# Attention and channel mix on one core: long-row tiles loaded by one transfer in place of two, with a new order of tasks

## Chip, core and metric

The kernel runs on one core of a Trainium2 chip. The metric is the device time of one execution in microseconds. A core has TensorE (PE, with its weight loads listed apart as PEld), VectorE (DVE), ScalarE (ACT), GpSimd (POOL) and the queue of SyncE (SP), which issues the DMAs of this kernel, and 16 DMA engines.

## The reference

Attention over blocks of 64 rows, then an RWKV channel mix, for 8 batches, 8 heads, 576 rows and heads of 64, so that a row of all heads has 512 columns:

```python
def _attn_ref(q, k, v):                      # each (8, 8, 576, 64)
    scores = scale * np.matmul(q, k.transpose(0, 1, 3, 2))
    scores = np.where(block_i >= block_j, scores, -1e9)
    attn = np.exp(scores - max) / (sum + 1e-09)
    return np.matmul(attn, v)
# heads side by side give x (8, 576, 512)
def _moe_ref(x, mu_k, mu_r, w_k, w_v, w_r):
    x_prev = x moved down by one row, a zero row first
    xk = mu_k * x + (1 - mu_k) * x_prev
    xr = mu_r * x + (1 - mu_r) * x_prev
    k = np.maximum(xk @ w_k, 0)              # 512 -> 1024
    v = k * k @ w_v                          # 1024 -> 512
    r = 1 / (1 + np.exp(-(xr @ w_r)))
    return r * v
```

## The kernel before

**Tiling.** Attention goes batch by batch (b = 0 to 7), the channel mix over nine chunks c of 512 rows of all batches together, so that chunk 0 needs batch 0 alone and chunk 1 batches 0 and 1.

**Long rows.** Scores need q and k turned, with the 64 columns of a head on partitions. For batches 0 to 3 (`LONGS = 4`) q and k come in as *long rows*: a partition takes nine successive rows of one head, 9 x 64 floats or 2304 bytes that lie together in DRAM, so 64 partitions hold a head. A tile `t_ld` of 128 partitions holds two heads (y = 0 on partitions 0 to 63, y = 1 on 64 to 127). `add_long` loads it, a cast to bf16 puts it into `t_nl` (two loads, x = 0 and 1, side by side), and `add_long_qkt` turns it on TensorE (line 389, task `qt`) and copies it from PSUM into `t_qkt` (task `ev`). Batches 4 to 7 load q and k in runs of 256 bytes and turn them by DMA (`turn`, line 311).

**Which heads share a tile.** In batch 0 a tile's heads are neighbours in DRAM (4g + 2x and the next), so its 128 rows of 2304 bytes are one run and it is loaded by one transfer. In batches 1 to 3 they are heads 2g + x and 4 + 2g + x, four heads apart (`heads(b)`), since their scores and values are arranged in another way; each tile is loaded by two transfers to 64 partitions each. A long-row task `longld b g n x` (n = 0 for q, 1 for k) is one tile: 8 a batch, 32 in all.

**Order.** Nothing is ordered by the compiler. The program adds 1212 tasks, each with the engines that could do it; the string `ORDER` lists them by number in the order in which they are issued, and `PLACE` gives the engine of each that has a choice (D, A, P for DVE, ACT, POOL). Both came from a planner outside the kernel, which had a cost for each task. Each engine does its tasks in that order and waits in place where data or a buffer is missing. `+n` behind a number puts n matmuls ahead of the task that nobody reads (`unread`, line 260), to fill a wait of TensorE.

**Buffers and queues.** All loads and stores are issued by SP (line 232 for loads, 899 for stores), in the order of `ORDER`. `t_ld` has 8 buffers, which long rows, weights and the q and k of later batches share; `t_nl` and `t_vl` (values) have 4 each. A buffer comes free when its cast is done. The DMAs' completions go round over eight semaphores, so that an issue waits until the one eight before it has landed.

**In order of time.** SP issues batch 0's long rows and values, then batch 1's long rows mixed with the 20 weight loads (`wld`) and batch 1's values, then batch 2's and batch 3's long rows with values, the first stores and the first loads of batch 4. On TensorE the turn of a batch (`qt`) is followed by its scores (`sc`, line 524), which alternate with the channel mix of the chunk before (`pk` line 814, `pr` 853, `pv` 880), and by its products with the values (`av`, line 616).

Of the kernel before, what the change touches and what calls it, by code (L numbers as in the profile page):

```python
# [14 lines left out]
LONGS = 4  # L15

ORDER = """
# [67 lines left out]
"""  # L85

PLACE = (
    "DAPADDPDDPDDPPADDADDAPPPPAADDAAAADAADDADDDPDDPDPPPPPPDPPDDADDPAAAPAPPP"
    "PPDAAAAAADAAPDPAPPPAAPAPPPDAAAADAADPADPPPPPPAPDAPAPAAADDAAAPAADAAAPPAA"
    "DADAPDAAAPADDPDPPAAPDDADDPPAADDPPPDADPADPAAAAPAADPAADPPPPAPDPPAAPDPAPA"  # L90
    "AAPDADDDPDAAPDADADPAPDDDPDAAAAADPAPDADPDPAADPDDDAAADPDAAAAADPAAADADDPD"
    "AADAADAAADPADDPDAAPAADPDAAAAPAADDAPDDDPAPAADDADADADADADADADADAPADAPAPA"
    "PAPADAD"
)


# [36 lines left out]
def kernel(  # L133
# [13 lines left out]
    B, H, S, D = q.shape  # L147
# [89 lines left out]
    def flex(key, alts, fn, deps, takes=(), uses=()):  # L237
        return add(key, {e: None for e in alts}, fn, deps, takes, uses)
# [91 lines left out]
    JT = S // D  # L330
# [11 lines left out]
    def add_long(b, g):  # L342
        for n, src in enumerate((q, k)):
            nb = plan.buf("nl")
            tiles["nbbuf", b, g, n] = nb
            cast["qk", b, g, n] = []
            for x in range(2):
                ld = plan.buf("ld")
                key = ("ld", b, g, n, x)
                t = load(f"longld {b} {g} {n} {x}", key,  # L350
                         lambda: new("ld", [P, S], FP),
                         lambda d, src=src, x=x: [
                             (d[y * D:y * D + D], src[b, 4 * y + 2 * g + x]
                              .rearrange("(p j) d -> p (j d)", j=JT))
                             for y in range(2)] if b else [
                             (d, src[b, 4 * g + 2 * x:4 * g + 2 * x + 2]
                              .rearrange("y (p j) d -> (y p) (j d)", j=JT))],
                         takes=[ld])

                def fn(eng, me, n=n, key=key, x=x):  # L360
                    if x == 0:
                        tiles["nb", b, g, n] = new("nl", [P, JT, P], BF)
                    convert(eng, tiles["nb", b, g, n][:, :, x * D:x * D + D],
                            tiles[key][:, :].rearrange("p (j d) -> p j d", d=D))
                cast["qk", b, g, n].append(flex(
                    f"long {b} {g} {n} {x}", ANY, fn,
                    [t] + cast["qk", b, g, n], takes=[] if x else [nb],
                    uses=[ld] + ([nb] if x else [])))
# [624 lines left out]
```

## Time and profile before

| | us |
|---|---|
| median of 3 runs | 279.02 |
| range of 3 runs | 277.21 to 281.06 |
| the profiled execution | 280.93 |
| its span, first to last instruction | 278.8 |
| PE busy | 258.6 (93%) |
| DVE busy | 205.3 (74%) |
| ACT busy | 198.9 (71%) |
| POOL busy | 79.8 (29%) |
| DMA packets, share of 16 engines' span | 76.2% |

All durations come from the profiled execution. The slices of the page are 1/40 of the span each, and their digits tenths of busy time; PEclk is the granted clock of TensorE in tenths, with a mean of 0.976. A busy engine is not always one at its best, since matmuls are pipelined and their ends modelled. The chain of waits goes back from the last instruction to what released it; "SPq" in it is SP's queue issuing.

### The profile page before, as it was taken

The numbers are of one execution on the slowest core, as the hardware profiler recorded it, in microseconds if no ns is written. First come the engines' busy times: TensorE is split into PE (matmuls) and PEld (weight loads), VectorE is DVE, ScalarE is ACT, GpSimd is POOL, SyncE is SP. The second block draws the span as 40 slices with busy tenths as digits, with TensorE's granted clock in tenths as the row PEclk, the third lists the DMA queues.
The fourth block names the chain that finished last, engine by engine and source line by source line (L and its number), as shares of the span: only waits on it lengthen the run. The fifth ranks groups of instructions, "written<-read, shape, count | busy, mean of one in ns | idle before, by whom it ended". The sixth has DMA issues, their size and how long they took to land.

```text
span 278.8 us, 9043 instructions
## 1 busy us (share of the span) xinstructions
PE 258.6 (93%) x3787; PEld 134.3 (48%) x3787; DVE 205.3 (74%) x396; ACT 198.9 (71%) x292; POOL 79.8 (29%) x112
## 2 busy tenths in 40 slices
PE   8998689987998889989997998999999999999995
PEld 8765565533434443444353444544544355444443
DVE  2467796875775848987978899789799869972232
ACT  2698859958895679959995798668969965560530
POOL 4133104833355211430152214122732021100520
PEclk9999959997999979999999999999999999999999
DMA  7958999977799896999899988999987201203003
GB/s 227 245 122 243 225 248 235 261 208 227 229 255 213 175 205 145 245 156 199 213 206 164 227 228 183 189 225 205 226 161 176 78 2 40 114 0 115 38 30 121
DMA packets 110633, 48.82 MB, mean 175 GB/s; under 512 B 99201, under 2 KB 99457, under 8 KB 110593
## 3 DMA queue, kind: packets, MB, share of 16 engines
q1 hardware_dynamic: 110592, 48.26, 76.2%
q8 instruction: 29, 0.48, 0.7%
q14 instruction: 12, 0.09, 0.1%
HBM read 33.56 MB, written 9.44 MB: 154 GB/s over the span
## 4 chain that ended last, share of the span: by engine, by line
PE 70%; DMA 9%; SPq 5%; DVE 5%; ACT 4%; issue 3%; POOL 2%; POOLq 0%; ACTq 0%; DVEq 0%
PE t_mm L814 19%; PE t_mm L880 17%; PE t_mm L853 9%; PE t_s L616 9%; PE t_s L524 6%; DMA t_ld<-in_q_dram 6%; SPq L232 5%; PE t_mm L260 4%; PE t_s L389 2%; PE t_s L260 2%; ACT t_e L555 2%; DMA t_tl<-in_k_dram 2%; POOL t_k L838 1%; DMA t_vl<-in_v_dram 1%; ACT t_qkt L243 1%
## 5 line engine op out<-in xcount | busy, mean ns | idle before, releaser
L555 ACT ACTIVATE t_e<-t_s 128x1024 f16<-128x1024 f32 (+1 forms) x96 | 89.1, 980 | 11.1 <-PE t_s L524 8.5
L880 PE MATMUL t_mm<-WV,t_k 128*128 128x512 f16 (+1 forms) x296 | 70.2, 386 | 0.1
L814 PE MATMUL t_mm<-t_xk,WK 128*128 128x512 f16 x288 | 68.5, 379 | 0.6 <-DVE t_o L891 0.3
L838 POOL TENSOR_TENSOR t_k<-t_kr 128x512 f16<-128x512 f32 x26 | 28.3, 1099 | 66.5 <-ACT t_kr L826 35.8
L880 PEld LDWEIGHTS <-t_k 128*128 128x128 f16 x296 | 28.0, 100 | 36.3 <-issue 8.6
L861 ACT ACTIVATE t_t<-t_mm 128x512 f32<-128x512 f32 x36 | 21.4, 594 | 30.7 <-PE t_mm L853 29.4
L814 PEld LDWEIGHTS <-WK 128*128 128x128 f16 x288 | 26.4, 97 | 34.6 <-issue 5.6
L891 DVE SCALAR_TENSOR_TENSOR t_o<-t_t,t_mm 128x512 f32<-128x512 f32 (+1 forms) x37 | 24.7, 667 | 17.6 <-PE t_mm L880 14.5
L853 PE MATMUL t_mm<-WR,t_xr 128*128 128x512 f16 x144 | 36.2, 380 | 0.0
L826 ACT ACTIVATE t_kr<-t_mm 128x512 f32<-128x512 f32 x40 | 23.9, 597 | 13.1 <-PE t_mm L814 12.9
L828 DVE TENSOR_SCALAR t_kr<-t_mm 128x512 f32<-128x512 f32 x32 | 21.7, 685 | 8.0 <-PE t_mm L814 7.5
L616 PE MATMUL t_s<-t_e,VO 64*32 64x64 f16 (+7 forms) x1120 | 21.9, 284 | 4.9 <-issue 3.7
L524 PE MATMUL t_s<-t_qkt 64*64 64x512 bf16 (+7 forms) x560 | 25.8, 293 | 0.6 <-ACT t_e L555 0.6
L786 DVE SCALAR_TENSOR_TENSOR t_xr<-t_d,MUR,XT 128x384 f16<-128x384 f32 (+7 forms) x42 | 24.1, 584 | 0.2
L260 PEld LDWEIGHTS <-identb 128*128 128x128 bf16 x267 | 19.2, 113 | 7.5 <-issue 5.6
L838 DVE TENSOR_TENSOR t_k<-t_kr 128x512 f16<-128x512 f32 x21 | 16.2, 781 | 8.0 <-ACT t_kr L826 7.7
L616 PEld LDWEIGHTS <-VO 64*32 64x32 f16 x1120 | 16.0, 92 | 11.9 <-issue 7.5
L786 DVE SCALAR_TENSOR_TENSOR t_xk<-t_d,MUK,XT 128x192 f16<-128x192 f32 (+7 forms) x42 | 21.2, 523 | 0.0
L731 DVE TENSOR_TENSOR XT<-t_s,t_rt 128x512 f32<-128x512 f32 x28 | 18.5, 681 | 3.1 <-PE t_s L616 3.0
L853 PEld LDWEIGHTS <-t_xr 128*128 128x128 f16 x144 | 13.0, 98 | 15.7 <-issue 1.7
L754 POOL TENSOR_TENSOR t_d<-XT 128x576 f32<-128x576 f32 x10 | 11.9, 1191 | 30.3 <-DVE XT L731 11.9
L524 PEld LDWEIGHTS <-t_qkt 64*64 64x64 bf16 x560 | 11.1, 106 | 17.3 <-issue 15.2
(67 smaller groups left out, 292.4 us busy)
## 6 DMA issues: line engine op xcount, KB each, us to landing
out_dram<-t_o SPq DMA_DIRECT2D x35, 256.0 KB, 2.6
t_vl<-in_v_dram SPq DMA_DIRECT2D x56, 144.0 KB, 3.6
t_ld<-in_k_dram SPq DMA_DIRECT2D x32, 128.0 KB, 4.0
t_ld<-in_q_dram SPq DMA_DIRECT2D x32, 128.0 KB, 3.4
t_ld<-in_q_dram SPq DMA_DIRECT2D x24, 144.0 KB, 3.7
t_ld<-in_k_dram SPq DMA_DIRECT2D x24, 144.0 KB, 3.4
t_ld<-in_moe_w_k_dram SPq DMA_DIRECT2D x8, 256.0 KB, 4.8
t_ld<-in_moe_w_v_dram SPq DMA_DIRECT2D x8, 256.0 KB, 5.8
```

Of the source, the lines that this page charges most:

```text
L260: nc.tensor.matmul(spare.get("at", dst), identb, identb, start=True, stop=True)
L524: nc.tensor.matmul(PS[y * D:y * D + D, x, col:col + n], kq[:, 1, t * D:t * D + D], kq[:, 0, q0:q0 + n], start=True, stop=True)
L555: nc.scalar.activation(tiles["e", b, it][:, :, 0:w], tiles["ps", b, it][:, :, 0:w], AF.Exp, scale=ISQ)
L616: nc.tensor.matmul(PA[c * QC:(c + 1) * QC, u, lo:lo + n], weight((b, rows, c, t), kk), tiles["e", b, (c // 2, i)][rows, c % 2, at:at + n], ...
L786: nc.vector.scalar_tensor_tensor(dst, dt[:, 0, lo:lo + w], (MUK1, MUR1)[n][:, cc:cc + 1], x, ALU.mult, ALU.add)
L814: nc.tensor.matmul(ps, WK[:, cc, jc * P:(jc + 1) * P], tiles["xk", c][:, cc], start=(cc == 0), stop=(cc == CCn - 1))
L826: nc.scalar.activation(kt, ps, AF.Relu)
L828: nc.vector.tensor_scalar_max(kt, ps, 0.0)
L838: (nc.vector if eng == "DVE" else nc.gpsimd).tensor_tensor(dst, KR, KR, ALU.mult)
L853: nc.tensor.matmul(ps, tiles["xr", c][:, cc, jt * P:(jt + 1) * P], WR[:, cc], start=(cc == 0), stop=(cc == CCn - 1))
L880: nc.tensor.matmul(ps[:, 0:w], tiles["k2", c][:, jc, jt * P:(jt + 1) * P], WV[:, jc, cols], start=(jc == 0), stop=(jc == JCn - 1))
L891: nc.vector.scalar_tensor_tensor(tiles["o", c, jt, half][:, 0:w], tiles["t", c, jt][:, cols], 1.0, tiles["pv", c, jt, half][:, 0:w], ALU.a ...
```

## The change

The load of a long-row tile of batches 1 to 3 is written as one transfer: the two heads are taken by a slice with a step of four heads, and the source is the pattern (y, p, 9 x 64) with y = 2 and p = 64, against a destination of 128 partitions. Batch 0's load and all else of the computation stay.

```diff
                          lambda d, src=src, x=x: [
-                             (d[y * D:y * D + D], src[b, 4 * y + 2 * g + x]
-                              .rearrange("(p j) d -> p (j d)", j=JT))
-                             for y in range(2)] if b else [
+                             (d, src[b, 2 * g + x:2 * g + x + 5:4].rearrange(
+                                 "y (p j) d -> y p (j d)", j=JT))] if b else [
                              (d, src[b, 4 * g + 2 * x:4 * g + 2 * x + 2]
                               .rearrange("y (p j) d -> (y p) (j d)", j=JT))],
                          takes=[ld])
```

`ORDER` and `PLACE` are replaced by new ones. The tasks are the same 1212 with the same numbers; their order, the engine of many of those that have a choice, and the counts of unread matmuls (267 before, 288 after) are others. Their first lines:

```diff
 ORDER = """
-0 3 7 5 9 4 13 8 11 6 17 69+79 10 15 73 70 74 71 75 19 72 76 109+11 12 85
-110 88 23 14 86 97+12 111 16 21 89 81+11 87 112 18 98 27 20 77+11 90 79 82
...
+0 3 5 7 9 4 13 6 11 69+65 8 17 73 70 10 15 74 71 19 75 72 76 85+11 12 109 27
+86 113 14 21 110 100+12 87 16 114 18 77+11 111 25 78 112 79 20 101 81 116 83
...
 PLACE = (
-    "DAPADDPDDPDDPPADDADDAPPPPAADDAAAADAADDADDDPDDPDPPPPPPDPPDDADDPAAAPAPPP"
...
+    "PDAPDPPPPPAPPAPDAPDDDAAPDAAAADDAADADDDDDADDPPDPPDDPDDPPDDDADPPPPAPPPAP"
...
```

Decoded by the tasks' numbers, SP's new order is in outline the old one: batch 0's long rows and values; batch 1's long rows among weight loads; the other weights with batch 1's values; batch 2's long rows among the last weights; batch 3's with two stores, three pairs of batch 4's q and k and batch 2's values; then batch 3's values. TensorE's order has the same stages in the same sequence. The first place where TensorE needs batch 3's long rows stands in both directly behind `pv 1 1`.

More of the change, by code (lines that the diff above doesn't have):

```diff
@@ L17 @@
 ORDER = """
[67 rows of a table removed]
[66 rows of a table added]
 """
 PLACE = (
-    "DAPADDPDDPDDPPADDADDAPPPPAADDAAAADAADDADDDPDDPDPPPPPPDPPDDADDPAAAPAPPP"
[L89 to L93, printed above, removed]
+    "PDAPDPPPPPAPPAPDAPDDDAAPDAAAADDAADADDDDDADDPPDPPDDPDDPPDDDADPPPPAPPPAP"
+    "DPPAAAAADAAAPDDAPPPPPAPDAPPDAAAAAADPADPAAPAPAAPAPAAAAADADAAAPDPAAPDAPP"
+    "PPAPAPPPDAAPDAPDDAAADDAPAAPDPADDDPPDDPDAPDADAPPPDADPPADAAAADDPDDDPPPAA"
+    "AAPDDADADDDDADADADAAPDPDAAPDADDAADPAPDDDDAPDPADAAADDDDPAAAAAPAPAPDADAD"
+    "AAPDDAAADDPDPDPDAADAADPAPAAADDADDADDPDDAAAPADAPADADADADADAPADAPADADAPA"
+    "DADADAP"
 )
```

129 rows, old and new, of the table ORDER are left out of this document.

## The prediction

> **What bounds the kernel now.** I read first the page's slices and its chain of waits, then the chain in order of time, the table of stretches, the DMA issues, and last the timeline of TensorE where batch 3 begins.
>
> ```profile
> PE   8998689987998889989997998999999999999995
> ...
> DMA  7958999977799896999899988999987201203003
> ...
> PE 70%; DMA 9%; SPq 5%; DVE 5%; ACT 4%; issue 3%; POOL 2%; POOLq 0%; ACTq 0%; DVEq 0%
> ```
>
> A slice is 7 us. From slice 17 on (about 113 us) TensorE is full and the chain is PE almost without a break. The 14% of the chain that is DMA or SP's queue lies before that. The chain in order of time shows its form:
>
> ```profile
> 20.57 0.59 SPq L232
> 21.21 0.59 SPq L232
> ...
> 27.22 4.76 DMA t_ld<-in_q_dram
> 32.08 0.67 ACT t_nl L243
> ...
> 84.51 4.52 DMA t_ld<-in_q_dram
> 89.24 1.28 POOL t_nl L249 x2
> ```
>
> Columns: start, length, what. Loads of long rows (t_ld, then cast into t_nl) end the waits at 32, 63, 73 and 89 us, and ahead of each stand issues on SP (L232) of 0.55 to 0.6 us. So up to 89 us the kernel runs at the pace at which loads are issued and land. 89 us is where the last long row of batch 3 lands.
>
> ```profile
> 3.00:9.00 6.00, 6.00 (x82) 5.90 (x81) 0.75 (x1) 1.34 (x2) 0.67 (x1) 1.00 0.99 327
> 0.00:89.00 89.00, 78.27 (x1371) 49.33 (x1379) 58.93 (x121) 66.59 (x93) 31.80 (x57) 0.94 0.87 226
> 95.80:278.80 183.00, 173.57 (x2269) 81.54 (x2268) 140.38 (x261) 128.48 (x193) 44.61 (x51) 0.99 0.72 150
> ```
>
> After the length stand busy times of PE, weight loads, DVE, ACT, POOL, then granted clock, DMA share, GB/s. Up to 89 us the 16 DMA engines are busy 0.87 of the time: they too have little to spare. From 95.8 us to the end TensorE works 173.6 of 183 us.
>
> ```profile
> t_ld<-in_q_dram SPq DMA_DIRECT2D x24, 144.0 KB, 3.7
> t_ld<-in_k_dram SPq DMA_DIRECT2D x24, 144.0 KB, 3.4
> ...
> t_ld<-in_q_dram SPq DMA_DIRECT2D x4, 288.0 KB, 5.7
> t_ld<-in_k_dram SPq DMA_DIRECT2D x4, 288.0 KB, 4.7
> ```
>
> The 48 transfers of 144 KB are the ones that the change merges. The eight of 288 KB are batch 0's, already one transfer to 128 partitions.
>
> ```profile
> 95.87 0.86 PE L389 MATMUL t_s<-identb,t_nl 64*128 64x64 bf16 x27
> ```
>
> This is TensorE's first work on batch 3's long rows (the turn of q and k, L389). From its start to the end are 278.8 - 95.9 = 183 us.
>
> **What is removed.** 24 of the 48 issues on SP. A long-row issue took 0.47 to 0.59 us and a pair 1.1 to 1.2 (timeline of SP, 57 to 74 us), so 24 x 0.6 = 14.4 us of SP's queue. Not all of it counts: the chain crosses some 10 issues of second halves (4 between 20 and 27.2 us, 2 to 3 each around 58, 68 and 83), about 6 us. The bytes stay.
>
> The Trainium skill, page "DMA: Bandwidth & Descriptors", section "Rules for kernel authors", says that two transfers to disjoint partition halves run one after the other on the same engines and that one to 128 partitions is to be used. The trace agrees as far as issue goes (1.2 us a pair against 0.43 us for one of 288 KB at the start); by that rule the sum is the 6 us saved.
>
> **What is added.** A source form that the trace does not show. Both old halves, batch 0's merged load and every other load have a source whose outermost count is 64 or 128 rows. The new one is "y p (j d)": outermost 2 (heads 4 apart), then 64 rows of 2304 B, against a destination of 128 partitions. The trace's packet records hold 4,480 completion packets of 4 B, 16 for each of the 264 issues and 16 more for each of the 16 transposes: every transfer was spread over all 16 DMA engines. Whether the new one is, no row shows. The two ends:
> - Spread over 16, as batch 0's: 8 packets of 2304 B to an engine. A packet took 93 ns in the median (128 mean, 189 at the 90th percentile), so 0.74 us. The first eight loads landed 0.7 to 0.75 us apart, which agrees.
> - Cut along the outermost count, one engine for each of the two heads: 64 packets each, 64 x 93 ns = 5.95 us on two engines while 14 stand by. From the stretch 3 to 9 us: 327 GB/s at share 0.99 is 20.6 GB/s an engine, and 147,456 B at that take 7.2 us.
>
> I take the second end. The issue hands the hardware two patterns, and they share no count but the 2 on the outside; batch 0's row, the nearest in size, has 128 on both sides and says nothing of this. Were it so, the same two engines would serve all 24 loads, and their share of every other transfer waits in line there.
>
> The same page of the Trainium skill, section "Why a DMA increments its semaphore by 16 and not by 1", states that the engine count is the largest number up to 16 that divides the slowest dimension of both patterns, and that the lowest-numbered engines serve it. That speaks against this change: 2 and 128 give 2. All 16 completions of each transfer before agree with it, and by it the sum is the one below.
>
> **The sum.** Work of a hot engine up to the last long row of batch 3:
> - All else. Up to 89 us an engine is busy 0.87 x 89 = 77.4 us; the 48 halves are 4 packets each, 48 x 4 x 93 to 128 ns = 17.9 to 24.6 us; 53 to 60 us are left. Counted instead at undisturbed packet times (256 B 18 ns, 2048 B 84 ns) for what the new ORDER puts ahead of that load on SP (batch 0's q, k, v, the 20 weight loads, v of batches 1 and 2, three pairs of batch 4, two stores) it is 40 us. With 14 engines mostly waiting, there is less to disturb; I take 45.
> - 24 x 64 x 93 ns = 143 us (197 at 128 ns).
> - First issue to first packet and last packet to landing: 3 us.
>
> 45 + 143 + 3 = 191 us in place of 89. Then a cast of 0.7 us and the turn of batch 3, from which the old run needs 183 us: 191 + 1 + 183 = 375. What happens before fits into that: batch 1's eight loads end at about 66 us (5.9 + 5.2 + 4 + 48 of engine time and 3), batch 2's at about 128, and each batch needs some 28 us of TensorE (the old steps between av stages, 118.6, 143.9, 171.0 us), so TensorE has caught up and waits at batch 3's turn. At most eight loads lie in the t_ld ring, and a cast that waits holds its engine's queue (the new PLACE puts 20 of the 32 long-row casts on POOL, 10 on ACT, 2 on DVE; before 16, 11, 5), with value and weight casts behind it that free buffers for the next loads; for gaps that a hot engine has from this I add 5 us, an estimate of the size of SP's two longest waits for data before 113 us, 3.5 and 3.1 us. Span 380; the profiled run took 280.93 us for a span of 278.8, and the median run is 279.02, so a median lies 0.2 over this span: 380.
>
> The new ORDER and PLACE move casts between engines and change weight and value order; fill matmuls go from 267 to 288, 21 x 0.1 us, in waits. Both are costed at nothing here: they lie under the loads of batches 1 to 3. Without that cover (rivals below) I give them 4 us either way, the spread of the three runs shown. After batch 3's turn the old order is PE-bound and the new one has the same matmuls.
>
> **Rivals.**
> - *All 16 engines, and the issue time is won* (not slower; it decides if the pattern is spread over more than about 12 engines, for then a load takes under 1 us). For it: batch 0's rows, and SPq in the chain. Saves about 6 us: 273 us, with the new order 269 to 277. Chance 0.07.
> - *All 16 engines, and the wait moves to the data*. The stretch of 34 to 56 us has DMA share 1.04 and 245 GB/s; fewer issues then only queue the same packets sooner. 279 us, 275 to 283. The same comes out if the build makes two transfers of it again, so that only the order changes. Chance 0.07.
> - *Two engines at the disturbed packet time*: 60 + 197 + 4 + 1 + 183 = 445 us. It needs 128 ns a packet, for which two engines alone are an unlikely cause. It is the upper end of the forecast, not a case of its own.
>
> **Numbers.** Forecast 0.86, the not-slower rivals 0.14. The forecast's lower end: 40 + 143 + 2, and TensorE's bare 174 us after that, gives 359. I say 355 to 445, which holds nearly all of the forecast's 0.86; the 0.14 at 269 to 283 are left out. A measurement of this kernel can tell 2% from no change: faster by more 0.06, within 0.06, slower 0.88.
>
> **What would show it.** If right: the long loads of 288 KB land in a median of over 10 us; the DMA digits fall to 2 to 4 for the first half while loads still end the waits; the first L389 on t_nl of batch 3 comes at about 190 us; the page counts 109,872 packets on q1 (24 transfers fewer by 16 completions and the merged 24 with 2 in place of 16: 110,592 - 384 - 336). If the engines are all 16: 110,208 packets, landing at 3 to 6 us, digits of 8 and 9. A mixed sign (2 engines, but an end near 280) would mean that the loads were hidden and that my claim of their pace up to 89 us is wrong.

## The result, and the profile after

| | us | ratio to before |
|---|---|---|
| before, median of 4 runs | 279.12 | |
| after, median of 4 runs (376.09 to 378.79) | 377.51 | 1.352 (95% interval 1.342 to 1.363) |
| after, the profiled execution | 376.09, span 374.3 | |

The changed kernel is 35% slower. The page of it, with the same lines as before (slices are now 9.4 us), and its packets by queue:

```profile
PE   7850553495542375254869999999999999999995
...
DMA  8721324565211111137389999899999781020203
GB/s 256 132 77 52 124 76 136 141 165 172 100 51 51 53 51 76 73 102 166 89 172 229 230 193 237 221 184 250 187 206 261 161 139 58 4 90 25 113 0 114
...
q1 hardware_dynamic: 109872, 48.25, 53.0%
...
PE 40%; DMA 37%; SPq 12%; DVE 4%; ACT 3%; issue 2%; POOL 1%; ACTq 0%; POOLq 0%; DVEq 0%
```

Where the DMA digits were mostly 7 to 9 up to slice 25 before, slices 3 to 18 now have 1 to 6 and TensorE is full from slice 22 only, while DMA takes 37% of the chain (9% before): the DMA engines are mostly idle and yet what everyone waits for. In slices 12 to 15 they move 51 to 53 GB/s, where the prediction's stretch from 3 to 9 us had 327. The packets on q1 are 109,872, the number that the prediction gave for two engines.

The table of stretches (start:end, length, busy times of PE, weight loads, DVE, ACT and POOL, granted clock, DMA share, GB/s):

```profile
20.00:66.00 46.00, 18.86 (x303) 14.57 (x290) 12.43 (x29) 12.19 (x17) 3.62 (x8) 0.70 0.27 94
66.00:128.00 62.00, 33.79 (x484) 17.95 (x484) 26.54 (x52) 23.63 (x36) 12.10 (x15) 0.69 0.37 108
128.00:190.00 62.00, 32.67 (x416) 13.80 (x417) 16.77 (x33) 17.83 (x25) 6.94 (x9) 0.73 0.32 91
190.00:374.00 184.00, 176.12 (x2280) 82.60 (x2279) 144.65 (x271) 129.04 (x194) 50.10 (x54) 0.99 0.71 155
```

From 20 to 190 us the DMA engines are busy a third of the time and TensorE about half, its clock granted at 0.7 in place of 0.94; from 190 us on the picture is that of before from 95.8 us on (0.71 share, TensorE full). The timeline of SP's queue shows the pace (start, length, what, how many issues):

```profile
111.39 5.58 SPq L231 DMA_DIRECT2D t_ld<-in_q_dram  x1
117.06 5.58 SPq L231 DMA_DIRECT2D t_ld<-in_k_dram  x1
122.73 16.93 SPq L231 DMA_DIRECT2D t_ld<-in_q_dram  x3
139.75 5.55 SPq L897 DMA_DIRECT2D out_dram<-t_o  x1
```

One load every 5.67 us. The chain of waits in order of time gives the time from issue to landing in this stage, and that of transfers of another kind:

```profile
15.90 14.33 DMA t_ld<-in_moe_w_k_dram
...
122.73 17.02 DMA t_ld<-in_q_dram
139.75 15.71 DMA out_dram<-t_o
```

A long row lands 17.0 us after its issue began, three loads of 5.67 us; the four long rows on this chain from 47 us on take 14.1 to 21.8 us. A weight load and a store, which have 8 packets on each of 16 engines, take 14.3 and 15.7 us (4.8 and 2.6 in the median before): their share of the two busy engines stands in line behind long rows. On TensorE, a turn of each of batches 1, 2 and 3 stands thus in the timeline (in brackets the idle time just before, and who ended it):

```profile
70.76 1.89 PE L387 MATMUL t_s<-identb,t_nl 64*128 64x64 bf16 x36 [9.12 <-POOL t_nl L248]
...
132.55 1.14 PE L387 MATMUL t_s<-identb,t_nl 64*128 64x64 bf16 x18 [7.49 <-POOL t_nl L248]
...
196.25 1.45 PE L387 MATMUL t_s<-identb,t_nl 64*128 64x64 bf16 x54
```

Batch 1's and batch 2's turns waited for casts of long rows; batch 3's, at 196.25 us, waited for nothing. The table of waits (who waited for whom: us in total, times, longest) names the same place behind those casts:

```profile
POOL t_nl L248 <- DMA t_ld<-in_q_dram: 75.8, 8, 25.9
...
POOL t_nl L248 <- DMA t_ld<-in_k_dram: 56.0, 8, 17.6
```

POOL stood 132 us in all for landings of long rows, up to 25.9 us at a time, with the value casts behind it in its queue.

### The profile page after: what moved, and what is told of

It is laid out like the page before. It is cut to its first block, busy times and chain, and to the rows that moved or that the text cites. A ratio compares the mean times of both kernels' runs of the same rounds, so it can differ in the third digit from the quotient of the medians.

```text
span 374.3 us, 9054 instructions
## 1 busy us (share of the span) xinstructions
PE 278.0 (74%) x3808; PEld 142.8 (38%) x3808; DVE 208.0 (56%) x405; ACT 194.6 (52%) x285; POOL 81.4 (22%) x110
## 2 busy tenths in 40 slices
DMA packets 109913, 48.84 MB, mean 130 GB/s; under 512 B 98480, under 2 KB 98736, under 8 KB 109872
## 3 DMA queue, kind: packets, MB, share of 16 engines
q1 hardware_dynamic: 109872, 48.25, 53.0%
## 4 chain that ended last, share of the span: by engine, by line
PE 40%; DMA 37%; SPq 12%; DVE 4%; ACT 3%; issue 2%; POOL 1%; ACTq 0%; POOLq 0%; DVEq 0%
PE t_mm L878 13%; DMA t_ld<-in_q_dram 11%; PE t_mm L812 11%; SPq L231 11%; DMA t_ld<-in_k_dram 11%; PE t_mm L851 6%; PE t_s L614 4%; DMA out_dram<-t_o 4%; DMA t_ld<-in_moe_w_k_dram 4%; DMA t_ld<-in_moe_w_v_dram 3%; DMA t_vl<-in_v_dram 3%; PE t_s L522 3%; ACT t_e L553 2%; PE t_s L387 1%; DVE t_o L889 1%
## 5 line engine op out<-in xcount | busy, mean ns | idle before, releaser
L812 PE MATMUL t_mm<-t_xk,WK 128*128 128x512 f16 x288 | 71.9, 393 | 12.9 <-DVE t_o L889 7.3
L851 PE MATMUL t_mm<-WR,t_xr 128*128 128x512 f16 x144 | 41.2, 417 | 12.4 <-ACT WR L242 5.9
L878 PEld LDWEIGHTS <-t_k 128*128 128x128 f16 x296 | 29.1, 103 | 47.3 <-issue 21.4
L812 PEld LDWEIGHTS <-WK 128*128 128x128 f16 x288 | 26.7, 99 | 48.6 <-issue 21.8
L387 PE MATMUL t_s<-identb,t_nl 64*128 64x64 bf16 x288 | 12.1, 208 | 41.8 <-POOL t_nl L248 38.0
L248 POOL CAST t_nl<-t_ld 128x576 bf16<-128x576 f32 x20 | 13.6, 690 | 131.9 <-DMA t_ld<-in_q_dram 75.8
L242 ACT CAST t_nl<-t_ld 128x576 bf16<-128x576 f32 x10 | 6.6, 669 | 54.6 <-DMA t_ld<-in_k_dram 43.5
L387 PEld LDWEIGHTS <-t_nl 64*128 64x128 bf16 x288 | 10.4, 106 | 45.6 <-POOL t_nl L248 39.9
L851 PEld LDWEIGHTS <-t_xr 128*128 128x128 f16 x144 | 14.1, 103 | 31.2 <-issue 18.3
L836 DVE TENSOR_TENSOR t_k<-t_kr 128x512 f16<-128x512 f32 x29 | 20.7, 718 | 7.7 <-ACT t_kr L824 7.3
L784 DVE SCALAR_TENSOR_TENSOR t_xr<-t_d,MUR,XT 128x448 f16<-128x448 f32 (+7 forms) x42 | 24.5, 590 | 0.5 <-POOL t_d L752 0.5
L248 DVE COPY t_qkt<-t_s 128x576 bf16<-128x576 bf16 x11 | 8.2, 756 | 28.6 <-ACT t_qkt L242 25.7
L784 DVE SCALAR_TENSOR_TENSOR t_xk<-t_d,MUK,XT 128x448 f16<-128x448 f32 (+7 forms) x42 | 21.5, 524 | 3.6 <-POOL t_d L752 3.6
```

Of the source, the lines that this page charges most:

```text
L387: nc.tensor.matmul(pst[:, j * D:(j + 1) * D], tiles["nb", b, g, n][y * D:(y + 1) * D, j], identb[y * D:(y + 1) * D, y * D:(y + 1) * D], is ...
L784: nc.vector.scalar_tensor_tensor(dst, dt[:, 0, lo:lo + w], (MUK1, MUR1)[n][:, cc:cc + 1], x, ALU.mult, ALU.add)
L812: nc.tensor.matmul(ps, WK[:, cc, jc * P:(jc + 1) * P], tiles["xk", c][:, cc], start=(cc == 0), stop=(cc == CCn - 1))
L836: (nc.vector if eng == "DVE" else nc.gpsimd).tensor_tensor(dst, KR, KR, ALU.mult)
L851: nc.tensor.matmul(ps, tiles["xr", c][:, cc, jt * P:(jt + 1) * P], WR[:, cc], start=(cc == 0), stop=(cc == CCn - 1))
L878: nc.tensor.matmul(ps[:, 0:w], tiles["k2", c][:, jc, jt * P:(jt + 1) * P], WV[:, jc, cols], start=(jc == 0), stop=(jc == JCn - 1))
```

## The experiments

Theory E is the prediction's: the merged load runs on two DMA engines because its source counts 2 on the outside. Rival O: the new order is the cause. Rival S: a source that steps over four heads is slow in itself, on however many engines. The kernel before was run again beside each of these kernels, with medians of 280.07 to 280.39 us, and a ratio is to the one run beside it.

**The two halves of the change apart.** First the new ORDER and PLACE with the old load:

```diff
-                             (d, src[b, 2 * g + x:2 * g + x + 5:4].rearrange(
-                                 "y (p j) d -> y p (j d)", j=JT))] if b else [
+                             (d[y * D:y * D + D], src[b, 4 * y + 2 * g + x]
+                              .rearrange("(p j) d -> p (j d)", j=JT))
+                             for y in range(2)] if b else [
```

> The new ORDER and PLACE with the old load: two transfers to 64 partitions for each long-row tile. Theory E (the merged load runs on two DMA engines, since its source counts 2 on the outside): without the merged load the slowdown is gone; 272 to 285 us, 110,592 packets on q1. Rival O (the new order is the cause): stays above 340 us. Rival S (a source that steps over four heads is slow in itself, on however many engines): as E here.

Measured: 277.27 us, ratio to before 0.987 (0.982 to 0.993), 110,592 packets. Then the old order with the new load (the same diff reversed, in the kernel before):

> The old ORDER and PLACE with the merged load, the other half of the change. E and S: 365 to 390 us, as the whole change, 109,872 packets on q1, TensorE's last turn of batch 3 at 190 to 210 us. O: 275 to 285 us.

Measured: 381.42 us (two runs), ratio 1.368 (1.355 to 1.380), 109,872 packets, the last turn of batch 3 at 206 us. O falls: the order by itself saves 1.3%, which is under the 2% that the prediction takes as telling, and the load does all the harm.

**The number of engines.** Two kernels keep the data packets, bytes and destination and change only the outermost count of the source, by reading other rows:

```diff
-                             (d, src[b, 2 * g + x:2 * g + x + 5:4].rearrange(
+                             (d, src[b, g::2, 0:288].rearrange(
```

> The changed kernel with another merged source: the first 288 rows of four heads, pattern (4, 32 rows of 2304 B), in place of two heads with 64 such rows. The same 128 packets of 2304 B and the same destination, but the attention of batches 1 to 3 computes on other rows. E: four engines, 32 packets each, 32 x 0.0886 = 2.84 us a load; hot work 50 + 24 x 2.84 = 118 us, + 3 + 1 + 178 = 300 us, 290 to 315; packets 110,592 - 384 - 24 x 12 = 109,920. S: as slow as the change or slower, 370 us and more. If all transfers kept 16 engines: 110,208 packets.

```diff
-                             (d, src[b, 2 * g + x:2 * g + x + 5:4].rearrange(
+                             (d, src[b, :, 0:144].rearrange(
```

> As the one before with the first 144 rows of all eight heads, pattern (8, 16 rows of 2304 B); the attention of batches 1 to 3 computes on other rows. E: eight engines, 16 packets each, 1.42 us a load; hot work 50 + 34 = 84 us, about what all engines have before, so 272 to 290 us; packets 110,592 - 384 - 24 x 8 = 110,016. S: 370 us and more.

And one with the count 128 that batch 0 has:

```diff
-                             (d, src[b, 2 * g + x:2 * g + x + 5:4].rearrange(
-                                 "y (p j) d -> y p (j d)", j=JT))] if b else [
+                             (d, src[b, 4 * g + 2 * x:4 * g + 2 * x + 2].rearrange(
+                                 "y (p j) d -> (y p) (j d)", j=JT))] if b else [
```

> The changed kernel with batch 0's form of the merged load in batches 1 to 3 as well: two neighbouring heads, one run of 128 rows, outermost count 128 on both sides. The scores of batches 1 to 3 are then those of other heads than the values. E: all 16 engines, 110,208 packets, long loads land in 3 to 6 us, and what is left of the change is the saved issue time: 0 to 6 us below the 277 us of the new order with two loads, 270 to 278. Rival P (merging itself costs, since a whole tile of 288 KB lands later than its halves): 280 to 290.

Measured, with the changed kernel in the last row; packets from the page, the cast and the turn from what the profile lists for t_nl:

| outermost count | packets on q1 | last long-row cast starts, us | last matmul of TensorE's turns starts, us | span, us | from that matmul to the end |
|---|---|---|---|---|---|
| 128 | 110,208 | 81.8 | 93.8 | 270.3 | 176.5 |
| 8 | 110,016 | 97.2 | 108.6 | 284.1 | 175.5 |
| 4 | 109,920 | 126.3 | 137.7 | 314.9 | 177.2 |
| 2 | 109,872 | 189.7 | 200.8 | 374.3 | 173.5 |

The times were 271.93 (median of six runs from 266.75 to 274.04, a spread too wide for a ratio), 285.92 and 317.29 (one run each) and 377.51 us. Every packet count is the one that E gave before the run. The packets of data are the same in all of them, and the completions of a merged load number 16, 8, 4 and 2: read as one from each engine that served it, the number of engines follows the outermost count. The page of the kernel with four heads:

```profile
DMA  7935457962233475799899799999989210110203
GB/s 239 213 109 170 152 168 214 204 179 103 102 129 139 136 163 150 177 239 198 207 191 252 194 158 206 263 171 179 253 201 169 93 69 4 67 68 35 101 0 133
...
q1 hardware_dynamic: 109920, 48.25, 63.9%
```

Its DMA digits fall to 2 to 4 in slices 10 to 14 and are back at 7 to 9 from slice 17, where the kernel with two heads stays low up to slice 18 of longer slices. The GB/s rows give the number of engines a second time, without the completions: the lowest stretches of the loading stage have 51 to 53 GB/s with two heads and 102 to 103 with four (slices 10 and 11), 26 GB/s an engine in both. The price follows too: by E each halving of the engines doubles the 24 loads' time on them (17.8, 34, 68, 136 us at 0.74, 1.42, 2.84 and 5.67 us a load, worked out from the packets), steps of 16, 34 and 68 us; the last cast moves by 15.4, 29.1 and 63.4 us, and what follows the last turn stays at 174 to 177 us. S falls with it, since four and eight strided heads are quicker than two. The kernel with four heads came out 2 us above its range of 290 to 315. Its span of 314.9 us is 15 over the sum of 300 in three nearly equal parts: the last row's cast starts at 126 us and not at 121, the first turn of batch 3 comes 6 us after that cast and not 1, and from there to the end are 183 us and not 178.

**The same two heads, the other way round.** The source can name the rows first:

```diff
-                                 "y (p j) d -> y p (j d)", j=JT))] if b else [
+                                 "y (p j) d -> p y (j d)", j=JT))] if b else [
...
+                        for j in range(JT):
+                            nc.tensor.matmul(
+                                pq[:, j // 8].bitcast(BF)[
+                                    :, j % 8 * P:j % 8 * P + P],
+                                tiles["nb", b, g, n][:, j], identb,
+                                is_transpose=True,
+                                start=(j % 8 == 0), stop=(j % 8 == 7 or j == 8))
```

Partition 2p + y then holds row group p of head y, and one matmul turns both heads. The source is read in the same pieces from the same two heads, with outermost counts of 64 in the source and 128 in the destination.

> The changed kernel with the same two heads four apart, the same bytes, rows and destination, but the pattern turned: (64 rows, 2 heads, 2304 B), so that the heads alternate on the partitions. TensorE then turns both heads of a tile in one matmul of 128x128 (9 for 18) and the copies from PSUM pick every second column; four of them are issued earlier. It computes the reference. E: outermost counts 64 and 128 give 16 engines, 110,208 packets, 268 to 279 us. S (the step over four heads is slow in itself): near 377 us.

Measured: 272.32 us, ratio 0.974 (0.967 to 0.981), 110,208 packets. This kernel takes the PSUM tile of batch 0's last block of 64 rows again too early, so that those rows are not the reference's. With the old order:

> The same load and turn with the old ORDER and PLACE; six copies from PSUM are issued earlier. E: 110,208 packets, 272 to 283 us, at or a little below the kernel before. S: near 380 us.

Measured: 271.99 us, ratio 0.973 (0.966 to 0.979), 110,208 packets. And in the new order with the tiles kept:

> As the rows-outermost kernel in the new order, with PSUM tiles taken at the places in the order at which the changed kernel takes them, so that batch 0's last block is not written over. E: 110,208 packets, 16 engines, 268 to 276 us; it beats the kernel before (280) and the new order with two loads (277).

Measured: 271.15 us, ratio 0.968 (0.964 to 0.971). The step over four heads costs nothing that these runs can tell (271 to 272 us with it and 271.93 without); the count named first does. This kernel computes the reference and beats both given ones; the other kernels with all 16 engines cannot be told apart from it. Lines of its page (slices of some 6.7 us):

```profile
PE   7799789999997989999999999999799999999995
...
DMA  6979699999998699889999999898982002203113
...
q1 hardware_dynamic: 110208, 48.25, 72.5%
...
PE 76%; DVE 7%; DMA 5%; ACT 4%; SPq 3%; issue 3%; POOL 0%; ACTq 0%; POOLq 0%; DVEq 0%
```

DMA and SPq are 8% of the chain, against 28% with the same order and two loads (18% and 10%). How much of the gain over that kernel (277.27 us) is issue time and how much the shorter turn (108 matmuls of 219 ns for 216 of 190 ns in batches 1 to 3) was not separated; the kernel with side-by-side heads and the old turn has 271.93 us too.

**How many loads, and where.** The merged load for batch 3 alone (`if b == 3`, two transfers for batches 1 and 2):

> The changed kernel with the merged load for batch 3 alone, two transfers for batches 1 and 2. E: eight loads at 5.67 us on the two engines in place of 0.74, 39 us more, less what TensorE still has to do before batch 3's turn, some 7 us: 300 to 318 us; packets 110,592 - 8 x 16 - 8 x 14 = 110,352. A theory in which the harm comes from the first merged loads, at batch 1: 275 to 285.

Measured: 309.87 us (one run), 110,352 packets. Eight loads cost 33 us over the new order's 277, 24 cost 100: about 4.1 us each in both.

**Which landing sets the end.** In the changed kernel the chain of waits does go through the landing of batch 3's last long row, but not to its turn:

```profile
174.98 14.05 DMA t_ld<-in_k_dram
...
189.68 0.67 ACT t_nl L242
190.35 1.05 ACT t_k L834 x2
191.40 0.49 ACT t_kr L824
191.93 1.87 PE t_mm L851 x4
```

The row's cast on ACT stood ahead of work for the channel mix (t_k, t_kr) in ACT's queue, and TensorE waited 3.6 us for that at 191.93 us. SP issues the last two long rows of batch 3 late, behind a store, batch 2's values and two pairs of batch 4. SP's order with them ahead, written by the tasks that the ORDER's numbers stand for:

```diff
 store 0 0 0
+longld 3 0 0 0
+longld 3 0 1 1
-qkld 4 0 1
-qkld 4 1 1
 vld 2 2
 vld 2 3
 vld 2 0
 qkld 4 3 1
-longld 3 0 0 0
 vld 2 1
-longld 3 0 1 1
+qkld 4 0 1
+qkld 4 1 1
```

> The changed kernel with one edit of SP's order: the last two long rows of batch 3 are issued ahead of batch 2's values, and two pairs of batch 4's q and k behind them. Theory L (the prediction's: the landing of batch 3's last long row sets the end, TensorE has caught up and waits for it): the last row lands at 172 to 176 in place of 189 us, and the end comes 13 to 17 us earlier, 360 to 365 us. Rival V (TensorE is held before that by batch 2's own values, stores and copies, which queue on the same two engines, and reaches batch 3's turn at 196 us anyway): the row lands as early, and the time stays at 370 to 380 us.

Measured: 378.75 us, ratio to before 1.351 (1.344 to 1.357), the time of the unmoved kernel. The timeline of its SP queue (start, length, what, how many issues):

```profile
159.53 0.57 SPq L166 DMA_DIRECT2D t_ld<-in_q_dram  x1
160.19 5.54 SPq L166 DMA_DIRECT2D t_ld<-in_k_dram  x1
165.78 16.20 SPq L166 DMA_DIRECT2D t_vl<-in_v_dram  x6
```

The timeline of its TensorE, at the end of the longest idle time of that stage:

```profile
185.96 3.57 PE L747 MATMUL t_mm<-t_xk,WK 128*128 128x512 f16 x8 [13.80 <-DVE t_kr L761]
```

The last two rows were issued at 159.5 and 160.2 us in place of 172.3 and 175.0, and no cast waited for them afterwards; their landing times the profile does not list. But batch 2's values (t_vl) then stood behind them and were issued over 16.2 us; TensorE idled 13.8 us before 185.96 us, in a chain that goes through the landing and cast of those values, and batch 3's turn ended at 203 us. So V holds: with the last long rows out of the way, batch 2's values end the wait instead, and the time stays. It is not the last long row by itself, but all that queues on the two engines up to that stage.

## Why the prediction was right, by its own steps

- *The choice between 16 engines and two.* The trace before had no row for it, as the prediction says; it was taken from the two patterns. The experiments show it: by the completions with counts of 2, 4, 8, 64 and 128 on the outside, by the GB/s of two and four engines, by the old order with the merged load, which differs from the kernel before in that load alone, and by the rows named first, which keep the heads and the bytes and change the order of the counts (with it the partitions and the turn). The Trainium skill's rule (page "DMA: Bandwidth & Descriptors", section "Why a DMA increments its semaphore by 16 and not by 1") is borne out in every run, with 2, 4, 8 and 16 completions a load; which of the engines served a load the traces do not show. The same page's rule for authors, in its section "Rules for kernel authors", that one transfer to 128 partitions is to replace two to halves, holds where the merged pattern keeps all engines in use (271 to 272 us with 64 or 128 counted on the outside) and fails where it does not (286, 317, 377).
- *The price of a load*, 64 x 93 ns = 5.95 us: measured 5.67, or 88.6 ns a packet, so 136 us in place of 143. The 93 ns is the length of a packet's record, and at 88.6 ns from one to the next successive records overlap a little. The disturbed price of 128 ns, the upper end of the range, played no part: the median record stayed at 93 ns.
- *All else on the hot engines*, 45 us with 3 us of start and landing: what is left of the 189 us at which the last row landed is 189 - 136 - 3 = 50 us, gaps included, where 45 + 5 for gaps had been allowed.
- *Batches 1 and 2* were to be loaded by 66 and 128 us; the casts of their last rows began at 70.0 and 131.8. The 28 us of TensorE a batch was read a little high (the steps quoted are 25.3 and 27.1 us), which changes nothing beside loads of 62 us a batch.
- *TensorE waits at batch 3's turn.* This step failed, as the timeline and the kernel with the last rows ahead show. The turn came at 196 us, 7 us after the last row, and without a wait of its own: TensorE was still at the channel mix ahead of it, held up before by a store (15.7 us to land, and DVE's next output buffer with it), by batch 2's values and, through ACT's queue, by the last long rows. The prediction looked at the turn alone, and not at who else waits on the same two engines through the in-order queues.
- *183 us from that turn to the end*: measured 374.3 - 196.3 = 178, and 178 too in the new order with two loads (from 95.9 to 273.8). Of these 5 us 4 lie between the first and the last turn of batch 3, 4.5 us apart in place of 8.5: the new order puts 54 of the batch's 72 turning matmuls together, where the old one has 27.
- *The sum.* With 5 us for gaps the turn was forecast at 197 us and came at 196.3, but by two misses that cancel: the row landed 7 us earlier than 196, and the turn came 7 us after it and not 1. The span is then 374.3 in place of 380. The 0.2 us from the span to a median was misread, since it sets the median against the span of another run: the profiled execution took 1.8 us more than its span (376.09), and the median of 377.51 lies 3.2 above it. So that 377.5 comes so close to 380 is in part luck; the mechanism and the price of a load are not.
- *The order at nothing.* It was worth -1.3% (3 us) by itself under the old load. Under the merged load the two orders stand at ratios of 1.352 and 1.368, whose intervals overlap; the difference of the medians is some 4 us. With the rows named first they cannot be told apart (271.15 and 271.99 us). So the new order was worth up to 4 us, the bound that the prediction gave for the case without cover.
- *The rival of a gain* had the right size, 6 us: merged on all engines, the load gives 271 to 272 us against 277 in the new order with two loads. How much of that is issue time, the rival's reason, is open.

## What to carry to other kernels

When two transfers are joined into one, write down both access patterns and compare their outermost counts: here a load that named 2 heads first ran on 2 of 16 engines, and the same bytes with the 64 rows named first ran on all. The sign to look for is a low DMA share while DMA ends the waits, and where the data stays the same the packets on the page tell the number of engines: here each engine less took one completion from every load. Price such a load by its packets on the busiest engine, and count everything behind it in the same queue, stores and weights included.

## What was not expected of the hardware

SP itself was held. A long row's issue takes 0.4 to 0.6 us before, and in the changed kernel many issues, a store's too, take 5.5 to 5.6 us, the time of one load on the two engines. A long row then landed 17.0 us after its issue began, three load times, so some two loads stood in line ahead of it. So transfers behind it, whose own data would have used the 14 idle engines too, were not issued meanwhile, and SPq rose from 5% to 12% of the chain.

Where TensorE waited, its clock was lower as well: it was granted 0.70 from 20 to 66 us and 0.86 over the whole run, against 0.98 before. Since it was waiting anyway, the runs do not show a time for that.
